# A two-layer decode kernel on one core: a fifth load slot, a third score bank, a padded weight chunk, paired heads and an MLP in small steps

## The chip, the cores and the metric

The kernel runs on one core of one Trainium2 chip. The time is the device time of one execution in microseconds (us), as a median of several executions; the profile is of one execution. TensorE does matmuls and transposes, VectorE (DVE) and ScalarE (ACT) copy and reduce, GpSimd (POOL) sums across partitions, SyncE (SP) issues the loads. "PE" is TensorE's matmul row in a profile and "PEld" its weight loads, which overlap the matmuls.

All ratios below are the mean time of one kernel's fast runs over that of the kernel before in the same rounds on the same chip, so they are not quite the ratio of the medians that are quoted.

## The reference, cut to what matters

Code and diffs in this document are shortened: `...` marks what is left out, lines are joined, and the comments are mine.

```python
def _A_ref(x, k_cache, v_cache, wq, wo):          # B=8, 16 query heads, 8 KV heads, 4096 keys, Dh=256
    q = (x @ wq) -> [B, Hq, 1, Dh]
    scores = einsum("bhqd,bhkd->bhqk", q, k) * Dh**-0.5
    o = einsum("bhqk,bhkd->bhqd", softmax(scores), v)
    return o.reshape(B, 1, Hq * Dh) @ wo
def _B_ref(x, w1, w2, w3, w4): ...                # with one token the mixer part is zero; x + gelu(ln(x) @ w3) @ w4 is left
x = x + _A_ref(_layernorm(x), A_k_cache, A_v_cache, A_wq, A_wo)
x = x + _B_ref(_layernorm(x), B_w1, B_w2, B_w3, B_w4)
x = x + _A_ref(...)                               # the same caches and weights again
x = x + _B_ref(...)
```

Each KV head of a batch has 2.1 MB of K and 2.1 MB of V, and the two layers read the same caches. Every 128x128 piece of K or V is loaded into TensorE as a weight and meets only two query columns. So the kernel loads, transposes and multiplies at once, and any of loads, TensorE or waits can be the bound.

## The kernel before

A "head" below is one (layer, batch, KV head). K and V come in half-tiles of 1 MB through a ring of four slots. TensorE transposes each K half-tile in four groups of eight 128x128 pieces into PSUM, DVE and ACT copy them out, and TensorE multiplies each piece by the two query columns. Those two columns are repeated 32 times, so that a matmul has 64 columns; the copies are thrown away. Some transposed K half-tiles (nine of a batch's sixteen) stay in SBUF for the second layer, whose "kept" heads then load V alone (the fifth kept head also half of its K).

```python
N_RING = 4; N_KEEP = 9; N_REP = 32
...
# order, for each batch b: Dn(b-1), A(b+1): streamed; C(b): kept, layer 1; Bk(b+1): streamed, layer 0
for b in range(B):
    if b > 0:      seq += Dn(b - 1)
    if b + 1 < B:  seq += A(b + 1)
    seq += C(b)
    if b + 1 < B:  seq += Bk(b + 1)
...
def load_next():                                   # one half-tile, issued as its slot is freed
    ...
    t, r = ring[n % N_RING]
    op("sp", lambda e: e.dma_start(t[:, :, :], src[b, h].rearrange("(m s) d -> m s d", m=P)[:, a * HALF:(a + 1) * HALF, :]),
       writes=[r], dma=f"ring{n % N_RING}")
...
def kr(kc): return P if kc < 3 else 64             # D = 448: the fourth chunk of the rows has 64
last = e.matmul(mm[...], wq[0:kr(kc), kc, t * P:(t + 1) * P], lnT[0:kr(kc), kc, 0:n], ...)
...
scores(g); softmax_a(g); pv(g - 1)                 # two score banks; each scores() also pumps one MLP step at a time
```

After a batch's last layer-0 head, its output projection, MLP and next queries ("the mix": 128 + 56 + 56 + 128 matmuls of one column) are spread over the next heads by `pump()`, one step a call; a step is up to 56 matmuls. The mix has to be finished before the batch's layer-1 heads start.

## Time and profile before

| | before |
|---|---|
| median | 1439.44 us (1435.59 to 1443.3, 2 runs) |
| loads | 472 MB; share of the DMA engines' time 84.0% |
| mean TensorE clock | 0.890 |

The page of the profile: the span cut in 40 slices, with the granted TensorE clock, the busy share of the DMA engines (tenths) and the rate; two DMA queues (packets, MB, share of the DMA engines' time); and, by engine, the chain of work that ended last.

```profile
span 1435.4 us, 55586 instructions
PEclk9879779978999799987999989997999779987696
DMA  5899749977999789986999879987999779995591
GB/s 220 319 403 397 298 178 417 404 289 284 390 411 367 274 348 376 401 316 230 403 395 405 308 289 392 411 347 266 369 408 418 281 266 368 420 358 204 178 370 73
q1 hardware_dynamic: 70336, 471.97, 84.0%
q8 instruction: 202, 3.31, 0.9%
PE 48%; DMA 38%; DVE 7%; issue 5%; ACT 2%; POOL 0%; SPq 0%; POOLq 0%
```

Where the DMA digit is 9 and the rate about 400 or more, loads are the bound; every fourth slice or so drops to 200 to 300 GB/s. Three stretches of the middle show which stages those are, and they repeat from batch to batch. The columns are the window, its length, busy us of each engine with instruction counts, the mean clock, the DMA share and the rate. In order: a streamed stage (five heads), the mix stage (six streamed heads with the projections and the MLP of one batch), a kept stage (five heads).

```profile
231.90:283.70 51.80, 40.61 (x960) 38.19 (x960) 19.60 (x46) 18.49 (x35) 3.78 (x10) 1.00 1.01 412
283.70:362.00 78.30, 70.87 (x1456) 67.10 (x1456) 30.75 (x126) 19.47 (x40) 6.16 (x16) 0.83 0.78 296
362.00:397.00 35.00, 26.93 (x736) 25.29 (x736) 7.42 (x28) 8.75 (x25) 3.79 (x10) 1.00 1.00 389
```

The first is bound by loads, with TensorE idle for a fifth of it. The second is not: loads at 296 GB/s, TensorE busy for 90% and its clock at half for a third of the stage. The second costs most: 25.2 MB would take 61 us at 411 GB/s, and it takes 78.

The groups of the queries' matmuls, with different shapes kept apart (count, then busy us, mean ns):

```profile
L356 PE MATMUL mm<-lnT,wq_sb 128*128 128x1 bf16 x768 | 60.1, 170 | 11.4 <-DVE lnT L340 11.4
L356 PE MATMUL mm<-lnT,wq_sb 64*128 64x1 bf16 x256 | 46.1, 180 | 0.0
```

The mean durations look alike (170 and 180 ns), yet a quarter of the matmuls takes 43% of the busy time. Durations of pipelined matmuls overlap, so what counts is the distance from one start to the next: 25 to 37 ns between two 128-row matmuls, but 96 to 98 ns into and 107 to 116 ns out of a 64-row one.

### The profile page before, as it was taken

To read this page: it belongs to the slowest core of one execution; us is meant where nothing else is said; L and a number is where in the kernel's file an instruction comes from. 1 tells how busy PE (TensorE), PEld (TensorE's weight loads), DVE (VectorE), ACT (ScalarE), POOL (GpSimd) and SP (SyncE) were. 2 spreads that over 40 slices of the span, in tenths; PEclk is the share of its full clock that TensorE was granted. 3 is DMA by queue.
4 is the path that set the end of the run, shared out by engine and by line. 5 is a ranking of instruction groups with operands and counts; after the bars stand their busy time and mean duration, and the time that the engine had idled before them with its cause. 6 is when DMAs were issued, how large, how long until landed. Compare 5 with 4: busy or idle time off the path is not lost.

```text
span 1435.4 us, 55586 instructions
## 1 busy us (share of the span) xinstructions
PE 1150.1 (80%) x25832; PEld 1088.0 (76%) x25832; DVE 486.2 (34%) x1709; ACT 375.5 (26%) x803; POOL 113.4 (8%) x302
## 2 busy tenths in 40 slices
PE   2687878799788987789778897889877997887885
PEld 2677877788778887788777786778777887786874
DVE  1333413343234422343233522443233431334233
ACT  0233203322233222322233222421233222331030
POOL 0000010000100000000100101000100001000100
PEclk9879779978999799987999989997999779987696
DMA  5899749977999789986999879987999779995591
GB/s 220 319 403 397 298 178 417 404 289 284 390 411 367 274 348 376 401 316 230 403 395 405 308 289 392 411 347 266 369 408 418 281 266 368 420 358 204 178 370 73
DMA packets 70568, 475.52 MB, mean 331 GB/s; under 512 B 7216, under 2 KB 13120, under 8 KB 13568
## 3 DMA queue, kind: packets, MB, share of 16 engines
q1 hardware_dynamic: 70336, 471.97, 84.0%
q8 instruction: 202, 3.31, 0.9%
q14 instruction: 30, 0.25, 0.0%
HBM read 471.93 MB, written 0.01 MB: 329 GB/s over the span
## 4 chain that ended last, share of the span: by engine, by line
PE 48%; DMA 38%; DVE 7%; issue 5%; ACT 2%; POOL 0%; SPq 0%; POOLq 0%
DMA ring<-in_A_k_cache_dram 32%; PE tk L519 17%; PE ps L577 9%; PE ps L491 9%; DMA ring<-in_A_v_cache_dram 6%; PE mm L356 5%; PE mm L377 3%; PE mm L406 3%; DVE ktr L527 2%; ACT ktr L525 2%; PE mm L432 1%; DVE sm L309 1%; DVE sm L310 1%; DVE sm L312 1%; DVE sm L308 0%
## 5 line engine op out<-in xcount | busy, mean ns | idle before, releaser
L519 PE MATMUL tk<-ident,ring 128*128 128x128 bf16 x5888 | 473.1, 233 | 90.5 <-DMA ring<-in_A_k_cache_dram 87.9
L519 PEld LDWEIGHTS tk<-ident,ring 128*128 128x128 bf16 x5888 | 375.2, 105 | 103.3 <-DMA ring<-in_A_k_cache_dram 96.9
L577 PE MATMUL ps<-pT,ring 128*128 128x64 bf16 x8192 | 298.4, 196 | 43.2 <-DMA ring<-in_A_v_cache_dram 21.0
L577 PEld LDWEIGHTS ps<-pT,ring 128*128 128x128 bf16 x8192 | 277.5, 100 | 50.7 <-DMA ring<-in_A_v_cache_dram 27.4
L525 ACT COPY ktr<-tk 128x1024 bf16<-128x1024 bf16 x176 | 178.1, 1012 | 462.8 <-PE tk L519 462.8
L527 DVE COPY ktr<-tk 128x1024 bf16<-128x1024 bf16 x272 | 186.3, 690 | 241.1 <-PE tk L519 239.7
L491 PE MATMUL ps<-qT,keep 128*128 128x64 bf16 x4608 | 198.2, 197 | 37.9 <-ACT keep L525 18.9
L491 PE MATMUL ps<-qT,ktr 128*128 128x64 bf16 x3584 | 190.7, 203 | 43.8 <-ACT ktr L525 30.1
L491 PEld LDWEIGHTS ps<-qT,keep 128*128 128x128 bf16 x4608 | 170.3, 100 | 49.4 <-ACT keep L525 22.6
L491 PEld LDWEIGHTS ps<-qT,ktr 128*128 128x128 bf16 x3584 | 159.2, 105 | 56.7 <-ACT ktr L525 36.6
L525 ACT COPY keep<-tk 128x1024 bf16<-128x1024 bf16 x104 | 105.3, 1013 | 262.0 <-PE tk L519 262.0
L527 DVE COPY keep<-tk 128x1024 bf16<-128x1024 bf16 x184 | 123.8, 690 | 110.0 <-PE tk L519 108.4
L556 ACT ACTIVATE pT<-ps,nb 128x32 bf16<-128x32 f32 x256 | 77.1, 301 | 237.7 <-DVE nb L552 233.5
L561 POOL PARTITION_ALL_REDUCE dn<-rs x128 | 51.7, 404 | 749.5 <-ACT pT L556 749.5
L356 PE MATMUL mm<-lnT,wq_sb 128*128 128x1 bf16 (+3 forms) x1152 | 83.0, 173 | 26.7 <-DVE lnT L340 26.7
L586 DVE TENSOR_TENSOR oT<-ps,rc 128x4 bf16<-128x4 f32 x128 | 22.6, 176 | 241.2 <-PE ps L577 240.7
L544 DVE TENSOR_REDUCE pm<-ps 128x2 f32<-128x64 f32 x128 | 28.7, 224 | 213.6 <-PE ps L491 213.3
L356 PEld LDWEIGHTS mm<-lnT,wq_sb 128*128 128x128 bf16 (+1 forms) x1152 | 73.6, 104 | 35.3 <-DVE lnT L340 26.9
L546 POOL PARTITION_ALL_REDUCE gm<-pm x128 | 45.8, 358 | 444.7 <-DVE rc L585 342.5
L406 PE MATMUL mm<-lnT,w_sb 128*128 128x1 bf16 (+3 forms) x560 | 40.1, 172 | 22.5 <-DVE t L340 19.2
L406 PEld LDWEIGHTS mm<-lnT,w_sb 128*128 128x128 bf16 (+1 forms) x560 | 34.9, 102 | 27.8 <-DVE t L340 14.9
L556 ACT ACTIVATION_READ_ACCUMULATOR pT<-ps,nb 128x1 f32 x256 | 50.2, 196 | 0.0
(55 smaller groups left out, 308.1 us busy)
## 6 DMA issues: line engine op xcount, KB each, us to landing
ring<-in_A_v_cache_dram SPq DMA_DIRECT2D x256, 1024.0 KB, 7.9
ring<-in_A_k_cache_dram SPq DMA_DIRECT2D x184, 1024.0 KB, 7.5
wo_sb<-in_A_wo_dram SPq DMA_DIRECT2D x1, 3584.0 KB, 15.3
wq_sb<-in_A_wq_dram SPq DMA_DIRECT2D x3, 1024.0 KB, 11.1
w_sb<-in_B_w_dram SPq DMA_DIRECT2D x1, 1568.0 KB, 15.3
w_sb<-in_B_w_dram SPq DMA_DIRECT2D x3, 448.0 KB, 11.5
wq_sb<-in_A_wq_dram SPq DMA_DIRECT2D x1, 512.0 KB, 15.2
w_sb<-in_B_w_dram SPq DMA_DIRECT2D x1, 224.0 KB, 13.6
```

What stands on the lines that cost most here:

```text
L356: last = e.matmul(mm[:, C_Q + t * B:C_Q + t * B + n], wq[0:kr(kc), kc, t * P:(t + 1) * P], lnT[0:kr(kc), kc, 0:n], start=(kc == 0), stop=( ...
L377: last = e.matmul(mm[0:w, C_Y + c * B:C_Y + c * B + n], wo[:, t, c * P:c * P + w], oT[:, t // 2, t % 2, lo:lo + n], start=(t == 0), stop=( ...
L406: last = e.matmul(mm[:, C_H + t * B:C_H + t * B + n], w3[0:kr(kc), kc, t * P:(t + 1) * P], lnT[0:kr(kc), kc, 0:n], start=(kc == 0), stop=( ...
L491: last = e.matmul(pst[:, at:at + 2 * N_REP].rearrange("p (r j) -> p r j", j=2), kt(2 * i + c), repeated(qT[:, b, c, 2 * h:2 * h + 2]), sta ...
L519: last = e.transpose(bank[:, j * P:(j + 1) * P], src[:, i, c * P:(c + 1) * P], ident[:, :])
L525: op("act", lambda e, d=flat, s_=bank: e.copy(d, s_[:, :]), reads=[r_bank], writes=[r_kt])
L527: op("dve", lambda e, d=flat, s_=bank: e.tensor_copy(d, s_[:, :]), reads=[r_bank], writes=[r_kt])
L544: op("dve", lambda e: e.tensor_reduce(pm[q][0][:, :], pst[:, 0:2 * NI].rearrange("p (i j) -> p j i", j=2), axis=AX.X, op=ALU.max), reads=[ ...
L546: op("pool", lambda e: e.partition_all_reduce(gm[q][0][:, :], pm[q][0][:, :], P, ReduceOp.max), reads=[pm[q][1]], writes=[gm[q][1]])
L556: return e.activation(pT[q][0][:, :, :].rearrange("p i j -> p j i")[:, j, :], pst[:, 0:2 * NI].rearrange("p (i j) -> p j i", j=2)[:, j, :] ...
L561: op("pool", lambda e: e.partition_all_reduce(dn[q][0][:, :], rs[q][0][:, :], P, ReduceOp.add), reads=[rs[q][1]], writes=[dn[q][1]])
L577: last = e.matmul(pst[:, at:at + W_PV].rearrange("p (r j) -> p r j", j=2), v[:, i, c * P:(c + 1) * P], repeated(pT[q][0][:, a * HALF + i, ...
```

## The change

Its intent: keep the DMA queue filled (a fifth slot; transposing the first K before the queries exist), take away TensorE's waits on the softmax (a third score bank; the weighted sum of the last head goes ahead of the late scores), even out load-heavy and load-light heads (kept and streamed in turn), and make the mix cheaper and finer (zero-padded last chunk of wq and w3, one layernorm pass for both roots, steps of eight matmuls at a set rate). At the end, most of the last output projection is done before the last head is finished. The repeated columns go from 64 to 48 a matmul. It pays with one kept half-tile less. The core of the diff:

```diff
-N_RING = 4
+N_RING = 5
-N_KEEP = 9
+N_KEEP = 8
-N_REP = 32
+N_REP = 24
+N_PS = 3
...
+    op("dve", lambda e: e.memset(wq[64:P, 3, :], 0.0), writes=[r_wqz])
+    op("dve", lambda e: e.memset(w3[64:P, 3, :], 0.0), writes=[r_w3z])
...
-        seq += C(b)
-        if b + 1 < B:
-            seq += Bk(b + 1)
+        for i in range(kept_heads):
+            seq += C(b)[i:i + 1]
+            if b + 1 < B:
+                seq += Bk(b + 1)[i:i + 1]
...
+    def project(w, r_w, at, t0, t1_, n):
...
+                    last = e.matmul(mm[:, at + t * B:at + t * B + n], w[:, kc, t * P:(t + 1) * P],
+                                    lnT[:, kc, 0:n], start=(kc == 0), stop=(kc == KC - 1))
...
+        for t in range(0, 32, 2):
+            project(wq, wq_r, C_Q, t, t + 2, n)
             yield
...
+    def pump():
+        credit["n"] = credit["n"] + credit["rate"] if jobs else 0.0
+        while credit["n"] >= 1.0:
+            credit["n"] -= 1.0
+            step()
...
+            credit["rate"] = 1.4 if b in (0, B - 1) else 0.75
...
+    def attend(g):
...                                                  # the transposes and first scores of head g, then:
+        if g > 0:
+            pv(g - 1, 0)
...
+        for f in todo:
+            score(f)
+        softmax(g)
+        if g > 0:
+            pv(g - 1, 1)
```

## The prediction

> What bounds the kernel now. Two things take turns. In the streamed heads (five layer-0 heads, 21 MB) the stage table shows DMA share 1.00 to 1.01 at 408 to 412 GB/s, 10.2 us a head, TensorE with slack: memory-bound. While one batch's projections and MLP run (six streamed heads, 25.2 MB, ideal 61 us) it takes 77 to 80 us in the middle batches: DMA share 0.76 to 0.82, clock 0.81 to 0.85, PE busy about 88%. Kept heads take about 35 us for 11.5 MB (ideal 28; DMA share 1.00 at only 389 to 398 GB/s). At 411 GB/s the 475.5 MB are 1157 us; the other 280 us are: start (first 143 us carry 48 MB, 27 us lost, plus 26 in the stage after), about 18 us a batch in six MLP stages (about 108), about 7 us a batch in kept heads (about 45), about 46 in the last mix and kept stage, 25 of tail after the last attention output (chain of waits).
>
> Costs from starts of matmuls: transpose 56 ns; 64-column matmul 29 to 31 ns; one-column 25 to 37 ns; but entering and leaving a 64-row weight costs 96+107 ns at full clock, 98+116 at half.
>
> What the change does.
> - Padding: 46 tiles a batch, about 257 to about 120 ns each: about 6 us less TensorE a batch (18 to about 11-12 us).
> - Small steps spread that over eight heads, each with about 2.6 us of TensorE slack (10.2 minus about 7.6): it should fit. MLP-stage loss 18 to about 3 us a batch.
> - Third bank and late weighted sum remove the softmax wait; pairing kept and streamed heads gives 15.3 us of DMA for about 11 of TensorE: kept-head loss 7 to about 1 or 2.
> - Five slots and transposing K before the queries keep the start's queue filled: about 35 us of the 53 lost come back.
> - Tail: 16 instead of 128 output matmuls at the end, one all-reduce and one root instead of two: 25 to about 16 us.
> - Added: one kept half fewer, 8 x 1.05 = 8.4 MB, +20 us on the critical path, because all is then DMA.
> - End: the seven-batch MLP falls in four kept heads (5.1 us each) and makes them TensorE-bound, about 10 us lost.
>
> Clock. The clock record of the trace has two values, 1.0 and 0.5, in pieces of 3.413 us. "TensorE: Matmul & The Clock Gate" (the Trainium skill), Part 1, states the same. By my count of streamed columns per window, the clock fell only below about 0.37 of full streaming, and transposes counted. 48 instead of 64 columns (29 to perhaps 25 ns a matmul) save little and lower the count[...]. So I expect some half-clock windows inside streamed heads, mostly hidden by slack: mean clock 0.82 to 0.96.
>
> Sum: 484 MB at 408 = 1186, start 10, A1 stage 5, seven middle batches 7 x 3.5 = 25, end 10, tail and last head 18: 1254 us, rounded to 1250. Range 1218 to 1295. Faster by over 2%: 0.95; same 0.03; slower 0.02.
>
> Right if: span DMA share about 0.95 (was 0.84), about 384 GB/s mean; HBM read about 480 MB; chain of waits mostly ring loads; matmuls of wq and w3 without the 100 ns pairs; middle period about 142 us (was 164).
>
> Wrong if: the clock sits at 0.5 in long stretches, so that a streamed head takes 12 us of TensorE (transposes 107, others 40 to 53 ns) and the stages become TensorE-bound: near 1350. Or DVE, which waits in order for the all-reduces, holds evictions and TensorE idles on transposes' banks. Or the fifth slot brings less and HBM stays at 390 GB/s: +40 us.

## More of the kernel before

What TensorE waited for, in total over the run (us, times, longest); lines with "issue" are time in which it waited for nothing that the profile shows:

```profile
PE tk L519 <- DMA ring<-in_A_k_cache_dram: 87.9, 70, 8.4
PE ps L577 <- DMA ring<-in_A_v_cache_dram: 21.0, 30, 2.6
PE ps L577 <- issue: 20.2, 21, 2.1
PE ps L491 <- issue: 9.0, 8, 1.8
```

L519 are the transposes, L577 the weighted sum, L491 the scores. The "issue" lines are small here.

## The result, and the profile after

The median is 1285.12 us (1283.46 to 1286.78, 2 runs) against 1439.44: ratio 0.8928, 95% interval 0.8814 to 0.9042. That is inside the range, and 35 us above the centre of 1250. A run that turned out to be the same program again (e9 below) gave 1283.07 us in 3 rounds, ratio 0.8929 (0.8871 to 0.8986).

The same lines of the page of the kernel after:

```profile
span 1281.6 us, 56004 instructions
PEclk8889889899898978999899899899999998896696
DMA  9999889999999999999999899999999999996793
GB/s 350 388 415 418 340 341 418 399 358 365 396 420 396 367 374 417 415 380 369 416 418 408 346 394 420 417 395 389 387 414 418 373 371 376 412 391 261 253 377 142
q1 hardware_dynamic: 71488, 480.36, 93.9%
q8 instruction: 204, 3.34, 1.0%
PE 55%; DMA 23%; issue 13%; DVE 6%; SPq 1%; ACT 1%; POOL 1%; POOLq 0%; DVEq 0%
```

The start and most of the mix stages are mended. But the rate still falls to 340 to 390 GB/s in many slices where the DMA digit is 9. "Busy" here means that packets were under way, not that the engines were saturated. And in the chain that ended last, loads fell from 38% to 23% while "issue" rose from 5% to 13%.

The same kinds of stages, in order: a streamed stage (four heads), the paired stage (four kept and four streamed heads in turn), the mix stage (eight streamed heads).

```profile
83.60:122.50 38.90, 29.52 (x767) 27.94 (x764) 16.00 (x36) 15.68 (x32) 3.26 (x9) 1.00 1.01 419
325.00:389.90 64.90, 50.59 (x1344) 48.75 (x1342) 22.03 (x58) 21.24 (x47) 6.05 (x16) 0.92 1.01 408
389.90:474.10 84.20, 70.27 (x1840) 67.60 (x1840) 36.22 (x122) 27.43 (x54) 6.86 (x18) 0.90 0.96 373
```

The padded groups, all 128 rows now, and TensorE's waits:

```profile
L368 PE MATMUL mm<-lnT,wq_sb 128*128 128x1 bf16 x1024 | 44.2, 165 | 19.4 <-DVE lnT L356 9.8 <-issue 9.7
PE ps L617 <- issue: 71.5, 43, 3.1
PE ps L549 <- issue: 50.2, 42, 2.8
PE tk L525 <- DMA ring<-in_A_k_cache_dram: 49.3, 39, 6.1
PE tk L525 <- issue: 17.2, 20, 1.9
```

The 1,024 matmuls of the queries take 44 us where they took 106. Waits for K fell from 88 to 49 us. But L617 (weighted sum) and L549 (scores) now stand idle for 122 us "on issue", where the same two were at 29 before. In the timeline of TensorE in a paired stage (start, length, instruction, count, idle before it):

```profile
648.02 1.76 PE L549 MATMUL ps<-qT,keep 128*128 128x48 bf16 x64
649.62 0.56 PE L617 MATMUL ps<-pT,ring 128*128 128x48 bf16 x16
652.74 1.38 PE L617 MATMUL ps<-pT,ring 128*128 128x48 bf16 x48 [2.56 <-issue]
```

TensorE stops after the sixteenth matmul of a row of 64 with nothing to wait for, and goes on 2.6 us later.

**What the stops are.** The records of the DMA packets hold a queue of kind "instruction" (q8 in the page): 204 packets of 16,384 bytes in this run, which is 256 instructions of 64 bytes, and TensorE ran 52,176 matmuls and weight loads, which is 203.8 x 256. I put both lists side by side. Stops inside a run of one kind of matmul recur at multiples of 255.8 TensorE instructions, and they end 1.41 us (5 to 95%: 1.24 to 1.56) after one of these packets has landed, whatever the stop's length. So TensorE runs out of instructions and waits for its next block. The first row of the table counts every gap of more than 0.3 us, from one start to the next, that ends 1.1 to 1.7 us after a landing. That takes in gaps that end there by chance; the second row counts only those that also lie at a border between blocks (within 16 instructions of every 255.84th, counted from the 441st). In the kernel after, 104 of the 107 such gaps over 0.6 us lie within 8 instructions of a border.

| | before | after |
|---|---|---|
| stops on a block, by time alone | 64, 69 us | 126, 187 us |
| the same at a border | 36, 42 us | 123, 183 us |
| from reaching a block to the start of the next block's packet (median) | 2.8 us | 3.6 us |
| the packet itself (median) | 0.98 us | 1.02 us |
| from block to block (median) | 6.6 us | 6.1 us |

Below, stops are counted by time alone unless a border is named. The times of the kernel after add up: 3.6 + 1.0 + 1.4 = 6.0 us from one block to the next at the earliest. A block of scores and weighted sums is 128 matmuls of 25 ns, 3.2 us, so it stops for 2.8; a block with many 56 ns transposes takes longer than 6 us by itself and does not stop. The Trainium skill, "Runtime: NRT & Kernel Launch", section "Instruction fetch mechanics", describes such blocks of 16 KiB or 256 instructions and says: "The cost of crossing a 16 KiB boundary is one DMA tail-bump, mostly hidden." The size agrees with the trace; the second half does not hold here.

**By stage.** I took the end of each head's weighted sum as the stage's border, and split TensorE's time in each stage into streaming (gaps up to 0.4 us), stops on a block, and other waits. Means of five middle batches of the kernel after, per batch: the mix stage 85.1 us = 67.6 streaming + 15.2 stops + 2.4 other. Its loads alone would take 81.6 us at 411 GB/s. TensorE, with its stops, is the bound there, and it waits for loads hardly at all. The paired stage takes 64.6 us and its loads run at 405 to 418 GB/s. The kernel before had the same wait in its kept stages: 33 of its 42 us at borders are there, about 4 us of each stage of 35 us. In the prediction I put the loss of the kept heads down to the softmax wait and the uneven heads alone.

### The profile page after: what moved, and what is told of

The parts are those of the page before. It is cut to its first block, busy times and chain, and to the rows that moved or that the text cites. A ratio compares the mean times of both kernels' runs of the same rounds, so it can differ in the third digit from the quotient of the medians.

```text
span 1281.6 us, 56004 instructions
## 1 busy us (share of the span) xinstructions
PE 997.8 (78%) x26088; PEld 960.0 (75%) x26088; DVE 482.4 (38%) x1527; ACT 390.9 (31%) x811; POOL 105.4 (8%) x281
## 4 chain that ended last, share of the span: by engine, by line
PE 55%; DMA 23%; issue 13%; DVE 6%; SPq 1%; ACT 1%; POOL 1%; POOLq 0%; DVEq 0%
PE tk L525 24%; DMA ring<-in_A_k_cache_dram 19%; PE ps L549 13%; PE ps L617 11%; DMA ring<-in_A_v_cache_dram 4%; PE mm L368 3%; PE mm L394 3%; DVE ktr L532 2%; PE mm L442 1%; SPq L256 1%; DVE sm L317 0%; DVE sm L318 0%; DVE sm L335 0%; DVE sm L316 0%; ACT ktr L530 0%
## 5 line engine op out<-in xcount | busy, mean ns | idle before, releaser
L525 PE MATMUL tk<-ident,ring 128*128 128x128 bf16 x6144 | 503.7, 234 | 74.6 <-DMA ring<-in_A_k_cache_dram 49.3
L617 PE MATMUL ps<-pT,ring 128*128 128x48 bf16 x8192 | 263.8, 186 | 86.8 <-issue 71.5
L617 PEld LDWEIGHTS ps<-pT,ring 128*128 128x128 bf16 x8192 | 238.2, 98 | 93.9 <-issue 74.5
L532 DVE COPY ktr<-tk 128x1024 bf16<-128x1024 bf16 x320 | 217.6, 690 | 214.7 <-PE tk L525 214.3
L549 PE MATMUL ps<-qT,ktr 128*128 128x48 bf16 x4096 | 189.7, 187 | 23.4 <-issue 17.7
L549 PE MATMUL ps<-qT,keep 128*128 128x48 bf16 x4096 | 161.8, 188 | 34.5 <-issue 32.5
L549 PEld LDWEIGHTS ps<-qT,ktr 128*128 128x128 bf16 x4096 | 151.1, 99 | 28.6 <-issue 17.9
L549 PEld LDWEIGHTS ps<-qT,keep 128*128 128x128 bf16 x4096 | 140.7, 99 | 40.0 <-issue 36.7
L368 PE MATMUL mm<-lnT,wq_sb 128*128 128x1 bf16 (+1 forms) x1152 | 47.8, 165 | 22.0 <-DVE lnT L356 12.3
L394 PE MATMUL mm<-oT,wo_sb 128*128 128x1 bf16 (+3 forms) x1280 | 58.8, 169 | 7.5 <-issue 5.9
L368 PEld LDWEIGHTS mm<-lnT,wq_sb 128*128 128x128 bf16 x1152 | 42.2, 100 | 24.3 <-DVE lnT L356 13.7
L394 PEld LDWEIGHTS mm<-oT,wo_sb 128*128 128x128 bf16 (+1 forms) x1280 | 50.9, 106 | 11.9 <-issue 7.4
```

Of the source, the lines that this page charges most:

```text
L368: last = e.matmul(mm[:, at + t * B:at + t * B + n], w[:, kc, t * P:(t + 1) * P], lnT[:, kc, 0:n], start=(kc == 0), stop=(kc == KC - 1))
L394: last = e.matmul(mm[0:w, C_Y + c * B + lo:C_Y + c * B + lo + n], wo[:, t, c * P:c * P + w], oT[:, t // 2, t % 2, lo:lo + n], start=first ...
L525: last = e.transpose(bank[:, j * P:(j + 1) * P], src[:, i, c * P:(c + 1) * P], ident[:, :])
L532: op("dve", lambda e: e.tensor_copy(flat, bank[:, :]), reads=[r_bank], writes=[r_kt])
L549: last = e.matmul(pst[:, at:at + 2 * N_REP].rearrange("p (r j) -> p r j", j=2), kt(2 * i + c), repeated(qT[:, b, c, 2 * h:2 * h + 2]), sta ...
L617: last = e.matmul(pst[:, at:at + W_PV].rearrange("p (r j) -> p r j", j=2), v[:, i, c * P:(c + 1) * P], repeated(pT[q][0][:, a * HALF + i, ...
```

## The experiments

Three theories of what bounds the kernel after, and of where the missing 35 us are: **F**, blocks of instructions that come too slowly while loads fill the DMA engines; **C**, the half clock that 48-column matmuls bring about; **M**, plain matmul time. **G** is F without the loads' part in it. A caution: e1 and e2 compute a wrong attention and were still counted as correct, because the comparison with the reference is too coarse here to see it.

### e1: no loads

```diff
-        if n >= len(chunks):
+        if n >= N_RING:
             return
```

> The changed kernel, but only the first five half-tiles are ever loaded; every matmul, copy and wait on an engine stays, the result is wrong on purpose. Theory F (the 16 KB blocks of TensorE's own instructions arrive too slowly while the ring loads fill the DMA engines: about 6.1 us from block to block, 204 blocks): without loads the gap from entering a block to the start of the next block's transfer falls from a median of 3.6 us to under 1 us, block-to-block time to about 4.5 us, stalls after a block's landing from 187 us to under 40 us, and the span to about 880 to 950 us. Rival G (a block takes about 6 us whatever else runs): span stays near 204 x 6 = 1225 us, with no ring traffic at all. Rival C (half-clock and matmul time): the clock goes to 1.0, span about 900 us, but block-to-block stalls would not be what changes.

985.15 us (one run, so its state is unknown; no state on record here makes up the 300 us). The wait from reaching a block to its packet fell from 3.6 to 0.4 us, block to block to 4.4 us, stops from 187 to 7 us (8 of them; 3 at a border, 4 us). No "issue" line is left among the first six of TensorE's waits:

```profile
PE mm L368 <- DVE lnT L356: 17.2, 10, 4.0
PE tk L478 <- POOL ident L191: 11.4, 1, 11.4
PE mm L368 <- DVE t L356: 10.7, 3, 5.0
PE ps L549 <- DVE ktr L532: 7.7, 13, 1.1
```

G falls: it is the loads that make the blocks late. The span was longer than I expected (880 to 950), as TensorE also waits for the layernorm and for copies, as the lines show. An estimate from this trace: if each of its 202 measured blocks took its own time here, but never less than the 6.0 us seen with loads, the sum would be 1242 us; the same blocks took 1243 us in the kernel after. That fits F, but the 6.0 us is taken from the kernel that is explained, so it is no proof.

### e2: as much streaming in fewer instructions

```diff
-N_REP = 24
+N_REP = 60
-                for i in range(4):
+                for i in (0, 2):
-                for i in range(HALF):
+                for i in range(0, HALF, 2):
```

> The changed kernel with half as many score and weighted-sum matmuls, each of 120 columns instead of 48, so that two of 25 ns become one of about 52 ns: TensorE streams for as long as before with about 16,400 fewer instructions (about 64 of 204 blocks less); the result is wrong on purpose. Loads are all there. Theory F: span falls to about the DMA floor, 1195 to 1230 us, instruction-block stalls under 50 us. Rival M (TensorE's matmul time bounds it): unchanged, 1270 to 1290 us. Rival C (half clock): falls too, because the activity count rises, but then the run with 64 columns must fall as well.

1226.02 us, ratio 0.8536 (0.8472 to 0.86): 59 us less than the kernel after. Blocks 204 to 140, stops 187 to 24 us; only 3 of these 21 gaps, 2 us, lie at a border, the rest elsewhere in a block. In order, the paired and the mix stage of one batch:

```profile
309.00:375.00 66.00, 51.67 (x832) 49.16 (x832) 22.11 (x58) 21.24 (x47) 6.05 (x16) 0.92 1.01 415
375.00:452.00 77.00, 65.64 (x1328) 62.28 (x1328) 36.18 (x123) 27.43 (x54) 6.86 (x18) 1.00 1.01 415
```

The mix stage runs at 415 GB/s now, and TensorE waits for data again, as it should in a kernel bound by loads:

```profile
PE tk L525 <- DMA ring<-in_A_k_cache_dram: 105.7, 82, 5.6
PE ps L617 <- DMA ring<-in_A_v_cache_dram: 73.2, 67, 1.7
PE tk L525 <- issue: 0.7, 1, 0.7
```

Means of the same five batches: the mix stage 76.7 us = 65.3 streaming + 1.0 stops + 10.4 other; the paired stage 65.7, unchanged. A batch takes 142.5 us, where the kernel after takes 149.9. The clock rose too (0.94 against 0.89), so C is not excluded by this run alone; but clock and matmul time can act only through streaming, and in the mix stage that fell by 2.3 us a batch where the stops fell by 14.2 (and the other waits, for loads, rose by 8.0). M, which said "unchanged", falls as the whole cause.

### e3: 64 columns again

```diff
-N_REP = 24
+N_REP = 32
```

> The changed kernel with 64 columns in the score and weighted-sum matmuls as before the change (29 to 31 ns instead of 25). Theory F: matmuls are longer but blocks come at the same 6 us, so the time stays within 1 percent of 1285 us while the mean clock rises from 0.89 to about 0.95. Rival C (half clock caused by 48 columns costs the time): 1255 us or less. Rival M (matmul time): slower by 20 us or more.

1285.76 us, ratio 0.8944 (0.8883 to 0.9005): the same. The clock rose to 0.925, time at half clock fell from 272 to 193 us, and nothing came of it. Stops are at 168 us. So C falls in the form in which I expected it (64 columns win the 35 us back), and M's 20 us did not come either. What the longer matmuls and the higher clock do could cancel in part: streaming is up by some 45 us in all, in place of stops and other waits. What a higher clock is worth with the matmuls left alone was not tried.

### e4: loads in two halves of 64 partitions

```diff
-        op("sp", lambda e: e.dma_start(t[:, :, :], ...), writes=[r], ...)
+        w = P // 2
+        for i in range(2):
+            op("sp", lambda e, i=i: e.dma_start(t[i * w:(i + 1) * w, :, :], ...), writes=[r[i]], ...)
...                                                  # readers wait for both
```

> The changed kernel with each 1 MB half-tile loaded by two DMAs of 64 partitions (8 KB rows as before[...]), each with its own semaphore. Theory F with the block waiting its turn behind whole loads in the DMA engines: the wait from entering a block to its transfer falls from 3.6 us towards 2 to 2.8 us, block-to-block time from 6.1 to about 5.3 us, and the span to 1215 to 1255 us. If the wait is behind everything queued and not behind one load, nothing changes. Rivals C and M: no change, 1275 to 1295 us.

2015.72 us, ratio 1.3724 (1.3582 to 1.3865). I was badly wrong: a packet of 8 KB took 571 ns instead of 309. Two of the four runs, the profiled one among them, were slow; the fast ones took 1966 and 1982 us, and the ratio is theirs. The rate and the landing time (row: loads, size, us from issue to landing):

```profile
GB/s 249 241 243 234 230 230 235 234 236 232 245 244 232 228 245 245 233 230 230 238 237 227 233 236 252 260 238 234 234 230 257 240 225 228 228 231 226 227 212 137
ring<-in_A_v_cache_dram SPq DMA_DIRECT2D x512, 512.0 KB, 17.9
```

The wait of a block grew to 5.7 us along with the packets. From that I formed a new step of F: the wait is some ten packets long, so shorter packets should shorten it.

### e5, e6: shorter packets on all 128 partitions

```diff
-            t[:, :, :], src[b, h].rearrange(...)[:, a * HALF:(a + 1) * HALF, :]),
+            t[:, i * w:(i + 1) * w, :], src[b, h].rearrange(...)[:, a * HALF + i * w:a * HALF + (i + 1) * w, :]),   # w = HALF // 2, or // 4
```

> The changed kernel with each half-tile loaded by two DMAs of all 128 partitions and half the rows (4 KB packets instead of 8 KB). In the run of 64 partitions the packets took 571 ns instead of 309 and the wait of an instruction block grew from 3.6 to 5.7 us, so the wait looks like 10 to 12 packets whatever their length. Theory F: a 4 KB packet takes about 155 ns, the wait falls to about 1.8 us, block-to-block time to 4.5 to 5.7 us, stalls from 187 to under 70 us, loads run at 415 to 420 GB/s in the streamed stages and the span is 1205 to 1245 us. If the wait is set by bytes queued instead, nothing changes (1275 to 1295).

> The same in four DMAs of 2 KB packets. Theory F: wait about 0.9 us if packets take a quarter of 309 ns; span as with 4 KB packets or a few us less, unless packets of 2 KB have a cost of their own (over 77 ns each), which then costs bandwidth and shows as a lower rate in the streamed stages.

1311.93 us (ratio 0.9109) and 1365.12 us (0.9475). Packets of 4 KB took 159 ns and of 2 KB 85, so the best slices of the page reach 408 and 386 GB/s instead of 420; and the wait stayed where it was, 3.7 and 3.8 us. The step falls: the wait does not follow the number of packets.

### e7: the last weight chunk unpadded

```diff
-                    last = e.matmul(mm[...], w[:, kc, t * P:(t + 1) * P], lnT[:, kc, 0:n], ...)
+                    last = e.matmul(mm[...], w[0:kr(kc), kc, t * P:(t + 1) * P], lnT[0:kr(kc), kc, 0:n], ...)
```

> The changed kernel with the last weight chunk of wq and w3 at 64 rows again. It adds no instructions. My prediction counted 6 us of TensorE a batch for it. Matmul times alone: about 140 ns x 46 tiles x 8 = 50 us more TensorE time, so up to 1325 us where TensorE is the bound. Theory F: in the MLP stages the blocks come every 6 us whatever the matmuls take, so most of it hides in the stalls: 1285 to 1300 us.

1338.19 us, ratio 0.9283 (0.9236 to 0.9331): the padding is worth some 50 us. That is as much as my sum of matmul times, but it did not come about as that sum has it: TensorE's streaming grew by 97 us (the clock fell as well, from 0.894 to 0.864), and the stops fell by 60, from 187 to 128 us. F's number was wrong, and its mechanism half right, as the stages show. The first and the last mix, where the steps are dense and stops few (1.6 us and none in the kernel after), grew by 10.7 and 10.5 us. In the five middle batches the mix stage took 9.5 us more streaming and 6.2 us less stops, so it grew by 3.2 us only. That a stop can shrink only in blocks shorter than 6 us would explain why not all was hidden; it is argued, not shown.

### e8: four slots

```diff
-N_RING = 5
+N_RING = 4
```

> The changed kernel with four half-tile slots instead of five. With fewer loads queued the blocks may come somewhat sooner (in the kernel before, with four slots, the wait was 2.8 us at the median), but loads have less cover while TensorE stalls. Expected 1290 to 1330 us; if it is 1285 or less, the fifth slot bought nothing.

1330.63 us, ratio 0.9244 (0.9179 to 0.931): the fifth slot is worth about 45 us, though it makes the blocks later (wait 3.2 us with four slots; stops 103 us). TensorE's waits for loads are what came back: 119 us for K and 62 for V, against 49 and 15:

```profile
PE tk L525 <- DMA ring<-in_A_k_cache_dram: 119.3, 91, 6.5
PE ps L617 <- DMA ring<-in_A_v_cache_dram: 62.3, 61, 2.6
```

By stage, 25 us of it are in the seven paired stages (3.6 us each), some 8 in the mix stages together and some 8 at the start.

### e9: more instructions without more work

```diff
                     at = C_PV + W_PV * c
+                    if i % 4 == 0:
+                        e.nop()
...                                                  # and the same in the scores
```

> The changed kernel with 4,096 no-operation instructions strewn into TensorE's score and weighted-sum matmuls (one to every four): 16 more blocks of instructions, no more matmul time and no other column count. Theory F: the blocks still come about 6 us apart, so where they bound the kernel the time grows; with half of it bound by loads, 1320 to 1385 us, about 220 blocks, and matmuls that follow a no-operation keep their 25 ns or a few ns more. Rivals M and C: 1280 to 1295 us. If the matmuls after a no-operation start 100 ns later or more, the run tells nothing about blocks.

1283.07 us. This run tells nothing about F: it had 56,004 instructions and 204 blocks, exactly as many as the kernel after, so the no-operations never reached the chip. It counts only as a repetition of the kernel after.

### e10: at most two loads in flight

```diff
+        if n >= 2:
+            first.w = landed[n - 2]
-            writes=[r], ...)
+            reads=[first], writes=[r], ...)
```

> The changed kernel with a load issued only when the load two before it has landed, so at most two are in flight; the five slots stay. In three traces the wait of a block grew with the loads in flight when it was asked for: 2.5 us at 0.5 to 1 MB, 3.0 at 1 to 1.5, 3.75 at 1.5 to 2.5, 5.2 over 3. Theory F: the wait falls from 3.6 to about 3 us, block to block 6.1 to 5.7 us; the MLP stages gain up to 5 us a batch, and the streamed stages may lose rate (418 to about 405 GB/s). Span 1255 to 1295; I would not be surprised by no gain.

1545.32 us, ratio 1.0752 (1.0665 to 1.084), far outside what I expected. The blocks did come sooner: wait 2.0 us at the median, stops 67 us (22 at a border). But the loads fell to about 300 GB/s, which costs far more. (Take the wait, the stops and the rate as rough.)

### e11: kept and streamed heads not in turn

```diff
-        for i in range(kept_heads):
-            seq += C(b)[i:i + 1]
-            if b + 1 < B:
-                seq += Bk(b + 1)[i:i + 1]
+        seq += C(b)
+        if b + 1 < B:
+            seq += Bk(b + 1)
```

> The changed kernel with the four kept heads of a batch in a row and then the four streamed ones, as before the change. A kept head is 256 TensorE instructions, one block: about 6 us by theory F against 5.1 us of loads, and a streamed one 1.5 blocks, 9 us against 10.2. So about 1 us a kept head, 32 heads: 1305 to 1325 us. My prediction put the pairing, the third bank and the late weighted sum together at 5 to 6 us a batch (about 40 us).

1287.45 us, ratio 0.8965 (0.8907 to 0.9024): no difference. The paired stage became two, 65.3 us together on the mean of six batches against 64.6. The pairing bought nothing that can be told from noise.

### e12: large steps

```diff
-        for t in range(0, 32, 2):
-            project(wq, wq_r, C_Q, t, t + 2, n)
+        for t in range(0, 32, 8):
+            project(wq, wq_r, C_Q, t, t + 8, n)
...
-            credit["rate"] = 1.4 if b in (0, B - 1) else 0.75
+            credit["rate"] = 1.0
...                                                  # the other projections and the MLP likewise
```

> The changed kernel with the projections and the MLP in steps as large as before the change (whole output chunks, a quarter of the queries) at one step per call, padding kept. The MLP then falls in two or three heads instead of six. Expected 1305 to 1345 us, with longer half-clock stretches in the MLP stages; 1285 to 1295 if the small steps bought nothing.

1300.6 us, ratio 0.9054 (0.8997 to 0.9111), against 0.8929 (0.8871 to 0.8986) of e9 in the same rounds: the small steps are worth some 17 us, less than I expected. With large steps the first four heads of a mix stage take about 53 us (with loads at 302 to 325 GB/s) instead of 47, and the last four about 36 instead of 39.

## Why the prediction was right or wrong

- **The direction, the range and the bound before**: right. The mix stages and the start were the loss, and both shrank.
- **Start**: right. I expected 10 + 5 us lost in the first three stages; the first two carry 48.0 MB in 122.5 us, 5.7 us over 411 GB/s, and the third loses 8.6.
- **Added load of 8.4 MB**: right (HBM read 471.9 to 480.3 MB).
- **Padding, "about 6 us less TensorE a batch"**: the sum agrees (e7: some 50 us for eight batches), partly by luck. A middle batch gained about 3 us of it and the first and the last mix over 10 each, and the clock rose with it.
- **Tail**: right. From the last attention output to the end 17.3 us, was 24.8; I had said 16, and 18 with the last head.
- **Clock**: right as a range (0.894). That it costs little is not shown: e3 raised it, but with longer matmuls.
- **Middle batches, "7 x 3.5"**: a term that was mis-sized. By that term a middle batch is 58.7 MB at 408 GB/s plus 3.5 us, 147.4 us; it takes 149.9, so some 15 us more over six batches. (The period of "about 142 us" that I also named does not agree with my own sum.) The error is larger than it looks, as the loads proved faster than I took them for: 419 GB/s in the streamed stage, so 140 us a batch by loads alone, and the loss is nearly 10 us and not 3.5. The step that failed is "each with about 2.6 us of TensorE slack ... it should fit". I computed the slack from matmul starts alone. The mix stage has 15.2 us of stops on instruction blocks, which were about 1 us in the mix stages before, and they eat the slack of eight heads. With fewer instructions (e2) a batch takes 142.5 us, 2.4 over its loads.
- **End, "about 10 us"**: mis-sized. The last three stages lose 11.1, 18.9 and -6.2 us, 24 together, 14 more than I allowed. With the 15 of the middle batches that is nearly the whole 31 us between my sum of 1254 and the result. In e2 they lose 10.5, 11.5 and -7.3, so not all of it is stops; the rest is not settled.
- **"Third bank and late weighted sum remove the softmax wait; pairing ..."**: the pairing has no part in it (e11). What the third bank and the order of the weighted sum are worth was not tried alone.
- **The fifth slot**: I counted it only at the start and in the risks. It is worth 45 us (e8), most of it in the paired stages, whose gain I had put down to the bank, the order and the pairing. That this term came out near is luck.
- **The marks I had set**: the DMA share (0.939), the rate (378 GB/s), the HBM read and the end of the 100 ns pairs came about as I said. "Chain of waits mostly ring loads" did not: loads are 23% of the chain, PE 55% and "issue" 13%. Nor did the period of 142 us (149.9). These two pointed to the step that failed.

So the slack of the mix stage went into a wait that the kernel before hardly had there. e1 shows that the loads make the blocks late, e2 that this wait and not the matmul time holds the mix stage. That shorter matmuls use the blocks up sooner fits e3 and e7, where longer ones left less to wait (168 and 128 us of stops). How large the effect of an instruction block alone is, with everything else untouched, was not shown: e2 changed the clock as well, and e9 failed. What sets the length of the wait is open too. It is not the count of packets (e5, e6); in three traces (before, after, e8) it grew with the loads in flight (issued and not landed), from about 2 us with 0.5 to 1 load in flight to 3.0 to 3.8 us with 2 to 2.5. But their count alone does not set it: in e2 the wait is about 2.7 us with 2.5 in flight at the median, where the kernel after has 3.6 with 2.0. And cutting the loads in flight (e10) cost more than it gave. None of the kernels that are meant to compute the right result was faster than the kernel after; e2 suggests that up to 59 us more are to be had by whoever finds a way to do the work in fewer TensorE instructions.

## What to carry to other kernels

Count TensorE's instructions as a resource of their own: in an unrolled kernel with short matmuls and loads at full rate, divide them by 256 and compare that number of blocks, at the block-to-block time that the trace shows, with the span. A stop "on issue" that recurs every 256 instructions is that wait. Here only fewer instructions (e2) or no loads (e1) took it away, and longer matmuls at a higher clock (e3) gained nothing. Read a matmul's cost from start to start: a weight piece of another row count cost about 200 ns in and out although its duration looked like the others', and zero padding took that away; and test the parts of a change one by one, since here each of two parts (padding, slot) was worth 45 to 50 of the 154 us when taken away alone, the small steps some 17, and one (pairing) nothing.

## What the Trainium skill lacked or had wrong

- "Runtime: NRT & Kernel Launch", "Instruction fetch mechanics": it calls the crossing of a 16 KiB block mostly hidden. Here it cost TensorE 187 us of stops in 1282 (126 stops; 183 us at borders), 7 us without loads. That loads delay the blocks (0.4 us without them, 3.6 with them), and that TensorE resumes 1.4 us after a landing, no page that I read states.
- "TensorE: Matmul & The Clock Gate", "LDWEIGHTS (loading the stationary operand)": it says that a weight load's time depends on its columns alone, not on the rows. The durations agree (99 ns with 64 rows, 105 with 128). The section lacks what a change of rows costs: going from 128 rows to 64 and back took 96 + 107 ns from start to start, against 25 to 37.
- The same page, Part 4: it says that the full clock does not engage for transposes, which do not count as busy in the same way. In the kernel before, windows of 3.4 us with 26 transposes and only 8 other matmuls kept the full clock. In each window at full clock I counted the columns streamed, the transposes included. The 39 windows after which the clock fell had 3,052 at most, and the 277 after which it stayed had 2,912 at least, which is 0.37 to 0.39 of the 7,800 that 56 ns transposes would stream. Without the transposes the two groups overlap widely (up to 2,752 against down to 512). Part 1's two clock values and 3.413 us windows agree with the trace.
- "DMA: Bandwidth & Descriptors", "Rules for kernel authors": of two transfers to disjoint partition halves it says "Don't bother — they serialize". The advice holds, but the row gives no figure. Here packets of 8 KB to 64 partitions took 571 ns instead of 309, and the rate fell from about 410 to 235 GB/s (e4).
